# One scores episode per block, two-block first chunks and early weight quarters in a planned attention + MLP kernel

## The chip, the cores and the metric

The kernel runs on one core of one Trainium2 chip. The metric is the device time of one execution in microseconds (us), as the median of several executions, compared with the kernel before on the same chip. A profile's span is about 2 us shorter than the time of the execution. Engines are called as in the profile: PE (TensorE), PEld (its weight loads), DVE (VectorE), ACT (ScalarE), POOL (GpSimd), SP (SyncE, which issues most DMA).

## The reference, cut to what matters

```
B, H, S, D = 8, 8, 576, 64                     # d_model = H*D = 512
scores = q @ k^T / sqrt(D) + alibi;  window of 128 keys, causal
attn   = softmax(scores);  x = attn @ v        # [8, 576, 512]
xn     = (x - mean) / sqrt(var + 1e-6) * g_ln
out    = x + relu(xn @ w_ch1) @ w_ch2          # 512 -> 2048 -> 512
```

There are 4608 tokens, so 36 blocks of 128 tokens. The MLP needs 1152 matmuls with 512 moving columns; all that PE does besides is attention and transposes.

## The kernel before

Per block of 128 tokens: q, k and v are loaded as float32, cast to fp16 on POOL, transposed on PE (8 transposes, "T"), evicted (copied from PSUM to SBUF); scores are computed ("S"; an *episode* is a run of score matmuls with no other work of PE in it), ACT takes the exp, DVE multiplies with a decay mask, PE multiplies with v ("V"), DVE normalises and takes the layer-norm statistics and writes `xs`, PE transposes `xs` ("X") into the chunk's `xt`. Per chunk of four blocks: first layer ("A", 16 tiles of four matmuls), relu on ACT or DVE, second layer ("B", 4 tiles of 16 matmuls), residual, store.

The order of instructions on each engine is fixed when the kernel is built, by a list scheduler in the kernel itself (`Plan`). Every task has assumed costs and a priority; PSUM banks are acquired and released in the plan: four hold the scores (tile `sc`), four (`fb`) serve everything else. At run time each engine works its list in that order. The part that makes the scores:

```python
sc = psum.tile([P, 4, 512], FP32, tag="sc", name="sc")     # four banks, one tile
...
def e_s(half):                                             # 8 matmuls
    def emit(e, b):
        for slot in range(2):
            for side in (() if r == 0 else (0,)) + (1,):
                for g in range(2):
                    nc.tensor.matmul(sc[:, 2 * half + g, c0 : c0 + P], kt[rows, 1, hp, :],
                                     qkt[i][rows, 0, hp, :], start=True, stop=True)   # 64 rows
    return emit
sa  = add(f"Sa{i}", ("PE", 0.38), e_s(0), [ev] + prev, av(i, 2.0), acq=("sa", f"Sa{i}"))
sb_ = add(f"Sb{i}", ("PE", 0.38), e_s(1), [sa] + prev, av(i, 2.0), acq=("sb", f"Sb{i}"))
for half, s_ in ((0, sa), (1, sb_)):
    ...   # exp of that half on ACT: reads sc[:, 2*half : 2*half+2, :]
```

And the part that loads the weights, in four quarters each (float32 to fp16 in the DMA, issued by POOL):

```python
W_AFTER = {0: 4, 1: 8}       # w1 behind the loads of block 3, w2 behind those of block 7
```

The softmax here doesn't subtract the row's maximum and nothing guards it: scores larger than these inputs give would overflow.

## Time and profile before

| | before |
|---|---|
| time | 363.4 us (362.27 to 363.58, 3 runs) |
| span of the profile | 361.1 us |
| PE busy | 332.4 us, 92% |
| first MLP matmul | 34.15 us |
| PE waits for exp in its scores | 6.6 us, 22 times |
| four blocks in steady state | 37.18 us (X of blocks 20 and 24, at 181.88 and 219.06 us); 36.8 us as the mean of six chunks (first-layer starts at 75.15 and 295.70 us) |

The head of the profile page: busy time of each engine, then 40 equal slices of the span, each digit the busy share in tenths.

```profile
PE 332.4 (92%) x2672; PEld 173.4 (48%) x2672; DVE 216.7 (60%) x444; ACT 157.5 (44%) x237; POOL 78.8 (22%) x127
PE   1586999999999999999999999999999999999995
DVE  0578497667658666666657666765676667641011
DMA  9999999999996444564454346441000010002002
```

PE is full from the fifth slice on; what it is not doing lies in the first four slices (36 us), where the DMA engines are full. But a busy PE is not a PE at its peak: the Trainium skill, "Perfetto Trace Analysis", section "Identifying the Most-Contended Engine", calls matmul busy time no good measure of the distance to the roof, because matmuls are pipelined. So the spacing of starts has to be read. The waits of PE, longest in total first (line, waiting for what: us in total, times, longest):

```profile
PE fb L354 <- DMA iden<-iden: 7.3, 1, 7.3
PE sc L380 <- ACT probs L403: 6.6, 22, 0.6
PE fb L423 <- POOL vx L346: 3.1, 1, 3.1
```

The second line is the one that recurs. It is seen in the timeline of PE around one block's scores (start, length, engine, line, what; in brackets the idle time before and who ended it):

```profile
200.46 0.38 PE L519 MATMUL fb<-xt,w1sb 128*128 128x512 f16 x1
200.78 0.23 PE L380 MATMUL sc<-qkt,qkt 64*128 64x128 f16 x2
200.95 0.22 PE L380 MATMUL sc<-qkt 64*128 64x128 f16 x2
201.10 1.04 PE L519 MATMUL fb<-xt,w1sb 128*128 128x512 f16 x4
202.44 0.23 PE L380 MATMUL sc<-qkt,qkt 64*128 64x128 f16 x2 [0.30 <-ACT probs L403]
...
202.78 0.82 PE L519 MATMUL fb<-xt,w1sb 128*128 128x512 f16 x3
```

and of ACT in the same time:

```profile
201.38 1.02 ACT L403 ACTIVATE probs<-sc 128x1024 f16<-128x1024 f32 x1
202.94 1.02 ACT L403 ACTIVATE probs<-sc 128x1024 f16<-128x1024 f32 x1 [0.55 <-PE sc L380]
```

The planner put one first-layer tile (0.86 us of matmuls at 0.216 us each) between the two halves of the scores. PE is through with it at about 201.96 and stands until 202.44, because the exp of the first half, which reads banks 0 and 1 of the tile, ends at 202.40. (The 0.30 us in brackets is shorter because the profile models the ends of matmuls.) The second half writes only banks 2 and 3. The wait is made by the tile, not by the data (e3 below tests that).

### The profile page before, as it was taken

The page shows a single profiled execution, that of the slowest core. Times are in us where ns is not written, and L with a number is a line of the kernel's source. Part 1 is how long each engine was busy: PE and PEld are TensorE (multiplying, and loading weights), DVE is VectorE, ACT ScalarE, POOL GpSimd, SP SyncE. Part 2 cuts the span into 40 slices and gives each one's busy share as a digit, 9 for nine tenths or more (in the row PEclk, how much of TensorE's full clock was granted, in tenths as well). Part 3 has the DMA queues.
Part 4 walks back from the last instruction along what each step waited for, and adds up shares of the span by engine and source line. Part 5 has one row for each costly group of instructions (what it writes and reads, how often), then busy time and mean ns, then how long its engine had stood idle before and what let it go on. Part 6 is the DMA issues. An engine that isn't in the chain of part 4 may idle for free.

```text
span 361.1 us, 6732 instructions
## 1 busy us (share of the span) xinstructions
PE 332.4 (92%) x2672; PEld 173.4 (48%) x2672; DVE 216.7 (60%) x444; ACT 157.5 (44%) x237; POOL 78.8 (22%) x127
## 2 busy tenths in 40 slices
PE   1586999999999999999999999999999999999995
PEld 0364455545545545544554554555455555444442
DVE  0578497667658666666657666765676667641011
ACT  4253576245334542464245433653365335612700
POOL 4851541632112121112101211230111100000000
PEclk9999999999999999999999999999999999999999
DMA  9999999999996444564454346441000010002002
GB/s 169 226 194 212 218 196 208 201 230 224 234 186 196 93 88 124 142 115 93 122 134 93 89 118 145 119 89 56 33 29 2 29 61 31 0 31 87 0 33 86
DMA packets 122384, 42.75 MB, mean 118 GB/s; under 512 B 113392, under 2 KB 117616, under 8 KB 122352
## 3 DMA queue, kind: packets, MB, share of 16 engines
q1 hardware_dynamic: 118128, 38.12, 47.0%
q0 software_dynamic: 4224, 4.19, 7.0%
q8 instruction: 21, 0.34, 0.4%
q14 instruction: 11, 0.09, 0.1%
HBM read 37.06 MB, written 9.44 MB: 129 GB/s over the span
## 4 chain that ended last, share of the span: by engine, by line
PE 80%; ACT 12%; DVE 3%; POOL 2%; DMA 1%; issue 1%; SPq 0%; ACTq 0%; DVEq 0%
PE fb L519 32%; PE fb L545 32%; ACT probs L403 8%; PE sc L380 5%; PE fb L423 5%; PE fb L354 4%; PE fb L480 2%; ACT xt L490 2%; ACT ht L531 1%; DMA k<-in_k_dram 1%; DVE probs L409 1%; DVE xb L443 1%; POOL mmix L290 1%; POOL mnew L290 1%; DVE st L459 1%
## 5 line engine op out<-in xcount | busy, mean ns | idle before, releaser
L519 PE MATMUL fb<-xt,w1sb 128*128 128x512 f16 x576 | 140.7, 383 | 0.0
L545 PE MATMUL fb<-w2sb,ht 128*128 128x512 f16 x576 | 137.7, 379 | 0.0
L531 ACT ACTIVATE ht<-fb 128x512 f16<-128x512 f32 x118 | 70.4, 598 | 75.3 <-PE fb L519 75.1
L403 ACT ACTIVATE probs<-sc 128x1024 f16<-128x1024 f32 (+1 forms) x72 | 69.8, 974 | 37.2 <-PE sc L380 36.9
L519 PEld LDWEIGHTS <-w1sb 128*128 128x128 f16 x576 | 51.3, 98 | 52.9 <-issue 1.4
L545 PEld LDWEIGHTS <-ht 128*128 128x128 f16 x576 | 51.0, 98 | 52.3
L553 DVE SCALAR_TENSOR_TENSOR ot<-fb,rstd,xb 128x512 f32<-128x512 f32 x36 | 26.8, 748 | 46.4 <-PE fb L545 45.3
L346 POOL CAST vx<-v 128x512 f16<-128x512 f32 x36 | 22.6, 631 | 137.7 <-PE fb L423 128.9
L409 DVE TENSOR_TENSOR probs<-probs,mreg 128x1024 f16<-128x1024 f16 (+1 forms) x56 | 37.2, 666 | 24.8 <-ACT probs L403 24.4
L423 PEld LDWEIGHTS <-probs 128*128 128x128 f16 x544 | 26.9, 102 | 20.4 <-DVE probs L409 3.5
L490 ACT ACTIVATE xt<-fb 128x512 f16<-128x512 f16 x20 | 11.9, 597 | 55.1 <-PE fb L480 52.2
L337 POOL CAST q<-q 128x512 f16<-128x512 f32 x36 | 23.5, 653 | 57.1 <-issue 25.1
L380 PEld LDWEIGHTS <-qkt 64*128 64x128 f16 x544 | 19.4, 98 | 31.8 <-issue 24.7
L423 PE MATMUL fb<-vx,probs 128*128 128x65 f16 x544 | 29.9, 200 | 4.4 <-POOL vx L346 3.1
L529 DVE TENSOR_SCALAR ht<-fb 128x512 f16<-128x512 f32 x26 | 18.0, 692 | 24.1 <-PE fb L519 24.1
L380 PE MATMUL sc<-qkt,qkt 64*128 64x128 f16 x256 | 23.0, 229 | 9.4 <-ACT probs L403 6.6
L443 DVE TENSOR_TENSOR xb<-fb,rec 128x256 f16<-128x256 f32 x72 | 30.3, 423 | 2.1
L362 DVE COPY qkt<-fb 128x1024 f16<-128x1024 f16 x36 | 24.7, 686 | 10.4 <-PE fb L354 10.3
L470 DVE SCALAR_TENSOR_TENSOR xs<-xb,mv,g_t 128x512 f16<-128x512 f16 x36 | 28.3, 787 | 1.0
L380 PE MATMUL sc<-qkt 64*128 64x128 f16 x288 | 25.3, 229 | 0.8 <-DVE qkt L362 0.8
L459 DVE BATCH_NORM_STATS2 st<-xb 128x6 f32<-128x512 f16 x36 | 25.0, 694 | 1.1
L337 POOL CAST k<-k 128x512 f16<-128x512 f32 x36 | 23.0, 640 | 8.1 <-DMA k<-in_k_dram 8.0
(28 smaller groups left out, 135.8 us busy)
## 6 DMA issues: line engine op xcount, KB each, us to landing
out_dram<-ot SPq DMA_DIRECT2D x36, 256.0 KB, 2.1
q<-in_q_dram SPq DMA_DIRECT2D x32, 256.0 KB, 4.3
k<-in_k_dram SPq DMA_DIRECT2D x32, 256.0 KB, 4.6
v<-in_v_dram SPq DMA_DIRECT2D x32, 256.0 KB, 4.4
w1sb<-in_moe_w_ch_dram POOLq DMA_DIRECT2D x4, 512.0 KB, 10.9
w2sb<-in_moe_w_ch_dram POOLq DMA_DIRECT2D x4, 512.0 KB, 11.0
q<-in_q_dram SPq DMA_DIRECT2D x8, 128.0 KB, 3.7
k<-in_k_dram SPq DMA_DIRECT2D x8, 128.0 KB, 3.6
```

The costliest lines, as they stand in the source:

```text
L337: en.tensor_copy(out=dst[i][:, :], in_=s)
L380: nc.tensor.matmul(sc[:, 2 * half + g, c0 : c0 + P], kt[rows, 1, hp, :], qkt[i][rows, 0, hp, :], start=True, stop=True,)
L403: nc.scalar.activation(out=o, in_=n_, func=AF.Exp, scale=inv_sqrt_d)
L409: nc.vector.tensor_tensor(out=pv, in0=pv, in1=mask[:, 2 * half : 2 * half + 2, :, lo:], op=ALU.mult)
L423: nc.tensor.matmul(pp[:, hh * (D + 1) : hh * (D + 1) + D + 1], probs[i][:, bank, slot, side * P : side * P + P], vx[i - 1 + side][:, h, 0 ...
L443: nc.vector.tensor_tensor(out=xb[i][:, 256 * half : 256 * half + 256].rearrange("p (h d) -> p h d", d=D), in0=pp[:, :, 0:D], in1=rec[2 * i ...
L459: nc.vector.bn_stats(out=st[i][:, :], in_=xb[i][:, :])
L470: nc.vector.scalar_tensor_tensor(out=xs[i][:, :], in0=xb[i][:, :], scalar=mv[c][:, j, 0:1], in1=g_t[:, :], op0=ALU.subtract, op1=ALU.mult,)
L519: nc.tensor.matmul(fb[b][:, :], w1sb[:, kb, f * P : f * P + P], xt[c][:, kb, :], start=(kb == 0), stop=(kb == NKB - 1),)
L531: nc.scalar.activation(out=ht[c][:, f, :], in_=src, func=AF.Relu)
L545: nc.tensor.matmul(pm[:, :], ht[c][:, f, j * P : j * P + P], w2sb[:, f, :], start=(f == 0), stop=(f == NFB - 1),)
L553: nc.vector.scalar_tensor_tensor(out=ot[i][:, :], in0=fb[plan.held[key][1]][:, :], scalar=rstd[c][:, j : j + 1], in1=xb[i][:, :], op0=ALU. ...
```

## The change

Its intent: compute a block's scores in one episode of 16 matmuls into two PSUM tiles; start the MLP earlier with two chunks of two blocks; issue the weight quarters between the first blocks' loads; allow early casts to be shared among engines. Cut to its core:

```diff
-    NCHUNK = NBLK // CB
+    CHUNKS = [2, 2] + [4] * 8
-    sc = psum.tile([P, 4, 512], FP32, tag="sc", name="sc")
+    scs = [psum.tile([P, 2, 512], FP32, tag=f"sc{n}", name=f"sc{n}") for n in range(2)]
+    PICK = {}
-    W_AFTER = {0: 4, 1: 8}
+    W_AFTER = [2, 2, 3, 3, 4, 5, 6, 7]        # w1 quarters, then w2 quarters
+        (t_w1 if n < 4 else t_w2).append(dma(f"w{n}", "POOL", 0.8, 3.25, emit, loads[i][1], av(i, -60.0))[1])
-        c_eng = {"POOL": 0.62}
+        def pick(name, default, **cost):
+            return {e: cost[e] for e in PICK.get((name, i), default).split()}
-        sa = add(f"Sa{i}", ("PE", 0.38), e_s(0), ..., acq=("sa", f"Sa{i}"))
-        sb_ = add(f"Sb{i}", ("PE", 0.38), e_s(1), ..., acq=("sb", f"Sb{i}"))
+        s_ = add(f"S{i}", ("PE", 0.64 if r else 0.42), e_s, [ev] + prev, av(i, 2.0), acq=("sc", f"S{i}"))
```

Cut away: the mask copies on POOL get a later priority (they end up spread between the first casts), the planner prefers weight DMAs over loads and skips an engine where another would finish earlier, and the costs of small chunks are scaled; a few other assumed costs move by up to 0.1 us. `PICK` is empty, so no cast moves: all 108 of them are on POOL in both kernels.

More of the change, by code (lines that the diff above doesn't have):

```diff
@@ L101, in run @@
                     r, b = at(t)
-                    if r is not None:
-                        cand.append((max(r, f), t.v, t, b))
+                    if r is None:
+                        continue
+                    s = max(r, f)
+                    if any(max(r, free[o]) + c < s + t.eng[e] - 1e-9 for o, c in t.eng.items() if o != e):
+                        continue
+                    cand.append((s, t.v, t, b))
                 if not cand:
@@ L106, in run @@
                 s = min(c[0] for c in cand)
-                c = min((c for c in cand if c[0] <= s + 1e-9), key=lambda c: c[1])
+                c = min((c for c in cand if c[0] <= s + 1e-9), key=lambda c: (c[2].v > -9e3, c[2].ready) if e == "DMA" else c[1])
                 if best is None or (s, c[1]) < (best[0], best[1]):
@@ L163 @@
     CH = CB * P
-    NCHUNK = NBLK // CB
+    CHUNKS = [2, 2] + [4] * 8
+    FIRST = [sum(CHUNKS[:c]) for c in range(len(CHUNKS))]
+    CHUNK_OF = [c for c, n in enumerate(CHUNKS) for _ in range(n)]
     VD = D + 2
@@ L219 @@
     rec = ring("rec", 4, [P, 4], FP32)
-    sc = psum.tile([P, 4, 512], FP32, tag="sc", name="sc")
+    scs = [psum.tile([P, 2, 512], FP32, tag=f"sc{n}", name=f"sc{n}") for n in range(2)]
     fb = {n: psum.tile([P, 512], FP32, tag=f"fb{n}", name=f"fb{n}") for n in range(4)}
-    plan.banks["sa"] = [0]
-    plan.banks["sb"] = [1]
+    plan.banks["sc"] = [0]
     plan.banks["fb"] = list(fb)
@@ L247, in dma @@
         t = add(name + ".i", (eng, issue), emit, deps, v, lat=0.0)
-        return t, add(name, ("DMA", secs), None, [t], v, lat=2.0)
+        return t, add(name, ("DMA", secs), None, [t], -1e4 if eng == "POOL" else v, lat=2.0)
     def load(name, src, r, i, v):
@@ L286 @@
     for dst, lst, name in ((mmix, tmix, "mmix"), (mnew, tnew, "mnew")):
-        vv = av(3, 0.0) - 200
+        vv = av(2, 3.0)
         for hb in range(2):
@@ L297, in z3 @@
         nc.gpsimd.memset(mnew[0:HALF, :, :, 0:P], 0.0)
-    tmix += [add("z1", ("POOL", 0.6), z1, list(tmix), av(3, 0.1) - 200)]
-    tmix += [add("z2", ("POOL", 0.6), z2, tmix[:2], av(3, 0.1) - 200)]
-    tnew += [add("z3", ("POOL", 1.2), z3, list(tnew), av(3, 0.1) - 200)]
+    tmix += [add("z1", ("POOL", 0.6), z1, list(tmix), av(2, 3.1))]
+    tmix += [add("z2", ("POOL", 0.6), z2, tmix[:2], av(2, 3.1))]
+    tnew += [add("z3", ("POOL", 1.2), z3, list(tnew), av(2, 3.1))]
     loads, kept = {}, {}
@@ L309 @@
         )
-    W_AFTER = {0: 4, 1: 8}
+    W_AFTER = [2, 2, 3, 3, 4, 5, 6, 7]
     t_w1, t_w2 = [], []
-    for n in range(4):
+    for n, i in enumerate(W_AFTER):
         def emit(e, b, n=n):
-            nc.gpsimd.dma_start(out=w1sb[:, :, 512 * n : 512 * n + 512], in_=w1r[:, :, 512 * n : 512 * n + 512])
-        t_w1.append(dma(f"w1_{n}", "POOL", 0.9, 3.25, emit, loads[W_AFTER[0] - 1][2], av(W_AFTER[0], 0.5) - 300)[1])
-    for n in range(4):
-        def emit(e, b, n=n):
-            nc.gpsimd.dma_start(out=w2sb[:, 4 * n : 4 * n + 4, :], in_=w2r[:, 4 * n : 4 * n + 4, :])
-        t_w2.append(dma(f"w2_{n}", "POOL", 0.9, 3.25, emit, loads[W_AFTER[1] - 1][2], av(W_AFTER[1], 0.5) - 300)[1])
-    qkt_done, vx_done, aggr_done, xt_done = {}, {}, {}, {}
+            m = n % 4
+            if n < 4:
+                nc.gpsimd.dma_start(out=w1sb[:, :, 512 * m : 512 * m + 512], in_=w1r[:, :, 512 * m : 512 * m + 512])
+            else:
+                nc.gpsimd.dma_start(out=w2sb[:, 4 * m : 4 * m + 4, :], in_=w2r[:, 4 * m : 4 * m + 4, :])
+        (t_w1 if n < 4 else t_w2).append(dma(f"w{n}", "POOL", 0.8, 3.25, emit, loads[i][1], av(i, -60.0))[1])
+    qkt_done, vx_done, aggr_done, xs_done, xt_done = {}, {}, {}, {}, {}
     def attention(i):
@@ L338, in e_cast @@
             return emit
-        c_eng = {"POOL": 0.62}
-        cq = add(f"cq{i}", c_eng, e_cast(q16, q32), lq, av(i, 0.0))
-        ck = add(f"ck{i}", c_eng, e_cast(k16, k32), lk, av(i, 0.1))
+        def pick(name, default, **cost):
+            return {e: cost[e] for e in PICK.get((name, i), default).split()}
+        cq = add(f"cq{i}", pick("cq", "POOL", POOL=0.62, ACT=0.6, DVE=0.35), e_cast(q16, q32), lq, av(i, 0.0))
+        ck = add(f"ck{i}", pick("ck", "POOL", POOL=0.62, ACT=0.6, DVE=0.35), e_cast(k16, k32), lk, av(i, 0.1))
         q32.reads(i, cq); k32.reads(i, ck); q16.writes(i, cq); k16.writes(i, ck)
         def e_cv(e, b):
-            nc.gpsimd.tensor_copy(out=vx[i][:, :, 0:D], in_=v32[i][:, :, :])
-        cv = add(f"cv{i}", ("POOL", 0.66), e_cv, lv_, av(i, 0.2))
+            if e == "ACT":
+                nc.scalar.activation(out=vx[i][:, :, 0:D], in_=v32[i][:, :, :], func=AF.Copy)
+            else:
+                nc.gpsimd.tensor_copy(out=vx[i][:, :, 0:D], in_=v32[i][:, :, :])
+        cv = add(f"cv{i}", pick("cv", "POOL", POOL=0.64, ACT=0.62), e_cv, lv_, av(i, 0.2))
         v32.reads(i, cv); vx.writes(i, cv)
@@ L364, in e_ev @@
                 nc.scalar.activation(out=dst, in_=src, func=AF.Copy)
-        ev = add(f"ev{i}", {"DVE": 0.7}, e_ev, [tt], av(i, 1.2), rel=f"T{i}")
+        ev = add(f"ev{i}", pick("ev", "DVE", DVE=0.7, ACT=1.02), e_ev, [tt], av(i, 1.2), rel=f"T{i}")
         qkt.writes(i, ev)
@@ L369, in attention, with e_s @@
         prev = [] if r == 0 else [qkt_done[i - 1]]
-        def e_s(half):
-            def emit(e, b):
+        def e_s(e, b):
+            for half in range(2):
                 for slot in range(2):
@@ L380, in emit @@
                             nc.tensor.matmul(
-                                sc[:, 2 * half + g, c0 : c0 + P],
+                                scs[half][:, g, c0 : c0 + P],
                                 kt[rows, 1, hp, :],
@@ L386, in emit @@
                             )
-            return emit
         pr = []
-        sa = add(f"Sa{i}", ("PE", 0.38), e_s(0), [ev] + prev, av(i, 2.0), acq=("sa", f"Sa{i}"))
-        sb_ = add(f"Sb{i}", ("PE", 0.38), e_s(1), [sa] + prev, av(i, 2.0), acq=("sb", f"Sb{i}"))
-        for half, s_ in ((0, sa), (1, sb_)):
-            qkt.reads(i, s_)
-            if r:
-                qkt.reads(i - 1, s_)
+        s_ = add(f"S{i}", ("PE", 0.64 if r else 0.42), e_s, [ev] + prev, av(i, 2.0), acq=("sc", f"S{i}"))
+        qkt.reads(i, s_)
+        if r:
+            qkt.reads(i - 1, s_)
+        for half in range(2):
             def e_x(e, b, half=half):
                 o = probs[i][:, 2 * half : 2 * half + 2, :, lo:]
-                n_ = sc[:, 2 * half : 2 * half + 2, :].rearrange("p b (s c) -> p b s c", s=2)[:, :, :, lo:]
+                n_ = scs[half][:, :, :].rearrange("p b (s c) -> p b s c", s=2)[:, :, :, lo:]
                 if r:
                     o = o.rearrange("p b s c -> p b (s c)")
-                    n_ = sc[:, 2 * half : 2 * half + 2, :]
+                    n_ = scs[half][:, :, :]
                 nc.scalar.activation(out=o, in_=n_, func=AF.Exp, scale=inv_sqrt_d)
-            ex = add(f"ex{'ab'[half]}{i}", ("ACT", 1.03 if r else 0.62), e_x, [s_], av(i, 2.4 + half), rel=f"S{'ab'[half]}{i}")
+            ex = add(f"ex{'ab'[half]}{i}", ("ACT", 1.02 if r else 0.62), e_x, [s_], av(i, 2.4 + half), rel=f"S{i}")
             probs.writes(i, ex)
@@ L408, in e_m @@
                 pv = probs[i][:, 2 * half : 2 * half + 2, :, lo:]
-                nc.vector.tensor_tensor(out=pv, in0=pv, in1=mask[:, 2 * half : 2 * half + 2, :, lo:], op=ALU.mult)
-            pr.append(add(f"mk{'ab'[half]}{i}", ("DVE", 0.69 if r else 0.42), e_m, [ex] + t_mask, av(i, 3.0 + half)))
+                en = nc.vector if e == "DVE" else nc.gpsimd
+                en.tensor_tensor(out=pv, in0=pv, in1=mask[:, 2 * half : 2 * half + 2, :, lo:], op=ALU.mult)
+            pr.append(add(f"mk{'ab'[half]}{i}", pick("mk" + "ab"[half], "DVE", DVE=0.69 if r else 0.42, POOL=1.4 if r else 0.8), e_m, [ex] + t_mask, av(i, 3.0 + half)))
         vx_done[i] = cv
@@ L454, in attention @@
             nm.append(n_)
-        c, j = i // CB, i % CB
+        c = CHUNK_OF[i]
+        j = i - FIRST[c]
         def e_bn(e, b):
@@ L473, in e_xs @@
             )
-        xs_ = add(f"xs{i}", ("DVE", 0.69), e_xs, [ag, d_g], av(i, 6.6))
+        xs_ = add(f"xs{i}", ("DVE", 0.75), e_xs, [ag, d_g], av(i, 6.6))
         xs.writes(i, xs_)
+        xs_done[i] = xs_
         def e_tx(e, b):
@@ L490, in e_xt @@
                 nc.scalar.activation(out=dst, in_=src, func=AF.Copy)
-        xt_ = add(f"xt{i}", {"ACT": 0.6, "DVE": 0.45}, e_xt, [tx], av(i, 7.6), rel=f"TX{i}")
+        xt_ = add(f"xt{i}", pick("xt", "ACT DVE", ACT=0.6, DVE=0.45), e_xt, [tx], av(i, 7.6), rel=f"TX{i}")
         xt.writes(c, xt_)
         xt_done[i] = xt_
-        if j == CB - 1:
-            ag4 = [aggr_done[c * CB + n] for n in range(CB)]
+        if j == CHUNKS[c] - 1:
+            ag4 = [aggr_done[FIRST[c] + n] for n in range(CHUNKS[c])]
+            nb = CHUNKS[c]
             def e_ln(e, b):
-                nc.scalar.activation(out=lv[c][:, :], in_=mv[c][:, :, 1], func=AF.Ln, bias=eps_t[:, :])
+                nc.scalar.activation(out=lv[c][:, 0:nb], in_=mv[c][:, 0:nb, 1], func=AF.Ln, bias=eps_t[:, :])
             def e_rs(e, b):
-                nc.scalar.activation(out=rstd[c][:, :], in_=lv[c][:, :], func=AF.Exp, scale=-0.5)
+                nc.scalar.activation(out=rstd[c][:, 0:nb], in_=lv[c][:, 0:nb], func=AF.Exp, scale=-0.5)
             ln = add(f"ln{c}", ("ACT", 0.3), e_ln, ag4, av(i, 9.0))
@@ L505, in attention @@
             lv.writes(c, ln); lv.reads(c, rs); mv.reads(c, ln); rstd.writes(c, rs)
-            for n in range(CB):
-                mv.reads(c, xs_)
+            for n in range(nb):
+                mv.reads(c, xs_done[FIRST[c] + n])
             kept[c] = rs
     def mlp(c):
-        done = [xt_done[c * CB + n] for n in range(CB)]
+        nb = CHUNKS[c]
+        n_ = nb * P
+        done = [xt_done[FIRST[c] + n] for n in range(nb)]
+        v0, per = FIRST[c] / CB * SPAN, nb / CB * SPAN / 32
         relu = []
@@ L514, in mlp @@
             key = f"A{c}.{f}"
-            vm = c * SPAN + f * SPAN / 32
+            vm = v0 + f * per
             def e_a(e, b, f=f):
@@ L519, in e_a @@
                     nc.tensor.matmul(
-                        fb[b][:, :], w1sb[:, kb, f * P : f * P + P], xt[c][:, kb, :],
+                        fb[b][:, 0:n_], w1sb[:, kb, f * P : f * P + P], xt[c][:, kb, 0:n_],
                         start=(kb == 0), stop=(kb == NKB - 1),
                     )
-            a = add(key, ("PE", 0.864), e_a, done + [t_w1[f // 4]], vm, acq=("fb", key))
+            a = add(key, ("PE", 0.216 * nb), e_a, done + [t_w1[f // 4]], vm, acq=("fb", key))
             xt.reads(c, a)
             def e_r(e, b, f=f, key=key):
-                src = fb[plan.held[key][1]][:, :]
+                src = fb[plan.held[key][1]][:, 0:n_]
                 if e == "DVE":
-                    nc.vector.tensor_scalar(out=ht[c][:, f, :], in0=src, scalar1=0.0, scalar2=None, op0=ALU.max)
+                    nc.vector.tensor_scalar(out=ht[c][:, f, 0:n_], in0=src, scalar1=0.0, scalar2=None, op0=ALU.max)
                 else:
-                    nc.scalar.activation(out=ht[c][:, f, :], in_=src, func=AF.Relu)
-            r_ = add(f"r{c}.{f}", {"ACT": 0.6, "DVE": 0.69}, e_r, [a], vm - 4.0, rel=key)
+                    nc.scalar.activation(out=ht[c][:, f, 0:n_], in_=src, func=AF.Relu)
+            r_ = add(f"r{c}.{f}", {"ACT": 0.17 + 0.107 * nb, "DVE": 0.16 + 0.133 * nb}, e_r, [a], vm - 4.0, rel=key)
             ht.writes(c, r_)
             relu.append(r_)
-        for j in range(CB):
-            i = c * CB + j
+        for j in range(nb):
+            i = FIRST[c] + j
             key = f"B{i}"
@@ L539, in mlp @@
             for f0 in range(0, NFB, 4):
-                vm = c * SPAN + (16 + 4 * j + f0 / 4) * SPAN / 32
+                vm = v0 + 16 * per + (4 * j + f0 / 4) * SPAN / 32
                 def e_b(e, b, j=j, f0=f0, key=key):
@@ L556, in e_o @@
                 )
-            o = add(f"o{i}", ("DVE", 0.69), e_o, [last, kept[c]], vm - 4.0, rel=key)
+            o = add(f"o{i}", ("DVE", 0.75), e_o, [last, kept[c]], vm - 4.0, rel=key)
             ot.writes(i, o); rstd.reads(c, o); xb.reads(i, o)
@@ L566 @@
         attention(i)
-    for c in range(NCHUNK):
+    for c in range(len(CHUNKS)):
         mlp(c)
```

## The prediction

> **What bounds it now.** TensorE. The busy table gives PE 332.4 of 361.1 us (92%), DVE 60%, ACT 44%. The timeline shows two regimes. Until 34.15 us no MLP matmul runs: PE waits (waits of PE: 7.3 us for the identity, 3.1 for a POOL cast of v, 4.8 for DVE), while the stretches table shows the DMA engines full to 80 us. From then PE streams to 357.4; the tail after it is 3.7 us.
>
> In steady state four blocks cost 36.8 us (first-layer matmuls at 75.3 and 295.9 us, six chunks). 128x512 matmuls start 0.216 us apart, so 128 of them are 27.6. Per block the timeline shows transposes 0.45, probabilities times v 0.48, transposes of xs 0.23, and scores in two episodes of eight: each costs 0.34 plus a 0.1 gap on entry, and the second starts 1.2 to 1.34 us after a 0.86 us filler, because it waits for the first half's exp (22 waits of PE scores on ACT, 6.6 us). Both halves are in one PSUM tile, so the second write waits for a read of other banks.
>
> **What changes.** (1) Two tiles, 16 score matmuls in a row: estimated from these gaps 0.65 us instead of 1.10 to 1.26, so 0.5 us per block, all on the critical path. Some 27 blocks lie behind 75 us: 13 to 14 us. ACT then does two exps of 1.02 us back to back; DVE and four banks should carry the relus.
> (2) First chunks of two blocks: the first layer can start at about 21 us instead of 34.
> (3) Weight quarters come earlier, behind query casts. DMA is the limit here. Before, four quarters issued at 18.4 to 20.8 us landed 6.7 to 14.9 us later, about 3.6 us each, and a q load issued meanwhile took 15.0 instead of 4.5 us. The Trainium skill, "DMA: Bandwidth & Descriptors", section "Issuing engines are not separate DMA queues", says that such DMAs share 16 engines; this trace agrees. All weights (29 us) and eight blocks (3.55 us each) need until about 58 us. The instruction order has w2's last quarter issued only behind block 7's query cast, and the first two output tiles' last accumulation before the first four-block chunk. I expect that quarter near 57 us and that chunk's first matmul near 70 us, against 75.3 before, with 1.3 us less attention done: 3 to 4 us gained of the 13 us earlier start.
> (4) The shared casts do nothing: the table of picks is empty, all 108 casts stay on POOL. Its mask copies are spread, which brings block 1 forward 3 us.
>
> PE may run cold between waits: the Trainium skill, "TensorE: Matmul & The Clock Gate", "What's actually happening", says that the array runs at half clock after about 3.4 us idle. The trace agrees: first-layer matmuls at 34.3 us started 0.43 us apart. I allow 1 to 2 us.
>
> **Predicted: 345 us** (343 span + 2), range 336 to 353; faster by over 2%: 0.92, within 2%: 0.07, slower: 0.01.
>
> **Right if** waits of PE scores on ACT fall from 6.6 to under 1 us; a steady four-block period is 34.8 to 35.3 us; the first layer starts at 20 to 25 us; new PE waits of 8 us or more for w1, w2 or late loads appear before 60 us; 128x512 first-layer matmuls start at 67 to 73 us.
>
> **Wrong if** DMA shares loads and weights better (that chunk at 62 us: about 337); if doubled exps starve the bank evictions (period above 36: 352); or if entering and leaving score episodes costs less than I read.

## The result, and the profile after

The change took 346.7 us (345.6 to 347.81, 4 runs) against 362.95 us before in the same rounds. Ratios here are the mean time of one kernel's fast runs over that of the other's of the same rounds, so not quite the ratio of the medians: 0.9553, with a 95% interval of 0.9515 to 0.959. Timed again later in five rounds (e12 below) it took 347.97 us, ratio 0.9577 (0.9557 to 0.9597).

The head of the page after:

```profile
PE 321.2 (93%) x2736; PEld 177.8 (52%) x2736; DVE 217.1 (63%) x454; ACT 153.1 (44%) x245; POOL 80.7 (23%) x127
PE   1488788999999999999999999999999999999995
DVE  0885686897867666766676667666766676631011
DMA  9999999999999535644473456431100110011011
```

PE has 64 more matmuls (the small chunks) and 11 us less busy time, for the same work. Slices 5 to 7 (34 to 60 us) are less full than before. The waits of PE, all but four short ones:

```profile
PE fb L364 <- DMA iden<-iden: 7.1, 1, 7.1
PE fb L491 <- DVE xs L480: 4.5, 3, 2.3
PE sc L390 <- DVE qkt L372: 2.8, 5, 0.9
PE fb L432 <- DVE probs L418: 2.4, 2, 1.4
PE fb L534 <- DMA w1sb<-in_moe_w_ch_dram: 0.8, 1, 0.8
```

No line says that scores wait for ACT any more, and one wait of 0.8 us is all that PE is shown to spend on weights directly. One block's scores in the steady state, PE and then ACT:

```profile
199.56 0.39 PE L491 MATMUL fb<-iden,xs 128*128 128x128 f16 x4
199.88 0.23 PE L390 MATMUL sc<-qkt,qkt 64*128 64x128 f16 x2
...
200.28 0.22 PE L390 MATMUL sc<-qkt 64*128 64x128 f16 x2
200.43 2.76 PE L560 MATMUL fb<-w2sb,ht 128*128 128x512 f16 x12
```

```profile
200.48 1.93 ACT L411 ACTIVATE probs<-sc 128x1024 f16<-128x1024 f32 x2
```

The episode takes 0.65 us of PE (199.78, where the transposes end at 0.0556 us each, to 200.43), of which 0.10 is a gap on entry and 0.09 one on exit. Before, the two episodes and their gap took 1.24 us of it (2.00 us from 200.78 to 202.78, less the tile of 0.86, plus the first entry gap of 0.1). Both exps follow each other. Four blocks now take 34.89 us (X of blocks 18 and 22, at 155.09 and 189.98 us). Periods differ from block to block; over six chunks (first-layer starts at 71.05 and 279.34 us) the mean is 34.7 us against 36.8 before, which is 0.5 us per block.

**A ledger.** To see where time goes across kernels I use one derived number. Let work be the number of PE instructions started, each times its warm spacing read from the timeline: 0.2157 us for 512 columns, 0.108 for 256, 0.0556 for a transpose, 0.0344 for a score matmul, 0.0302 for one with v. It sums to 307.6 us in every correct kernel here. Lost time is elapsed time minus that work. The last column is part of the lost time and an estimate: the work that was started while TensorE ran at half clock, and so took about twice as long. It is taken from the clock records of each trace. Before a trace's first record there is none, and there transposes start 0.107 us apart in every run, so that time is counted as half clock too. It is an upper bound of what the half clock cost, because PE may have had to wait anyway. By stretch, in us:

| run | time, us | ratio to before (95%) | lost 0-20 | 20-40 | 40-80 | 80-300 | of it half clock |
|---|---|---|---|---|---|---|---|
| before | 363.4 | 1 | 16.9 | 11.2 | 3.6 | 16.5 | 9.5 |
| the change | 346.7 | 0.9553 (0.9515-0.959) | 16.3 | 8.2 | 5.3 | 3.1 | 6.7 |
| e12 the change again | 347.97 | 0.9577 (0.9557-0.9597) | 16.3 | 9.0 | 6.1 | 3.3 | 9.1 |
| e1 scores alone | 347.6 | 0.9577 (0.9559-0.9594) | 16.5 | 11.7 | 2.0 | 3.8 | 8.5 |
| e2 scores alone, one tile | 348.14 | 0.9582 (0.9567-0.9597) | 16.2 | 12.6 | 2.1 | 3.6 | 8.2 |
| e3 two tiles, two episodes | 353.54 | 0.9735 (0.972-0.9749) | 16.4 | 10.6 | 3.2 | 9.1 | 6.9 |
| e4 the start alone | 367.62 | 1.0117 (1.0094-1.014) | 17.2 | 9.3 | 9.1 | 17.6 | 7.8 |
| e5 change, chunks of four | 349.07 | 0.9607 (0.958-0.9633) | 16.3 | 14.7 | 1.1 | 3.2 | 8.5 |
| e6 change, late weights | 345.32 | 0.9503 (0.9479-0.9527) | 16.3 | 7.9 | 4.7 | 3.1 | 7.5 |
| e7 half weights (wrong result) | 346.1 | 0.9524 (0.9476-0.9573) | 16.3 | 9.0 | 5.3 | 3.2 | 8.5 |
| e8 weights first, four small chunks | 353.82 | 0.9731 (0.968-0.9781) | 16.9 | 7.2 | 11.9 | 4.4 | 9.0 |
| e9 half weights, planned (wrong result) | 342.73 | 0.9438 (0.9421-0.9455) | 16.3 | 4.8 | 4.5 | 3.6 | 3.7 |
| e10 change, ACT evictions | 347.88 | 0.9569 (0.9535-0.9602) | 16.9 | 8.8 | 4.4 | 3.2 | 6.3 |
| e11 late weights, ACT evictions | 345.27 | 0.9511 (0.9488-0.9533) | 16.3 | 6.9 | 6.4 | 2.9 | 6.4 |

The ledger of the change against before: of 16.6 us, 13.4 come from the steady stretch, 1.3 from what lies after 300 us (with the last blocks' scores), and 1.9 from all of the first 80 us, although the first layer begins at 22.62 us instead of 34.15. In e12, the same kernel timed again, it is 0.3 us, and its half-clock estimate is 2.4 us above that of the first profile: executions of one kernel differ by that much at the start.

### The profile page after: what moved, and what is told of

It is laid out like the page before. It is cut to its first block, busy times and chain, and to the rows that moved or that the text cites. A ratio compares the mean times of both kernels' runs of the same rounds, so it can differ in the third digit from the quotient of the medians.

```text
span 344.6 us, 6879 instructions
## 1 busy us (share of the span) xinstructions
PE 321.2 (93%) x2736; PEld 177.8 (52%) x2736; DVE 217.1 (63%) x454; ACT 153.1 (44%) x245; POOL 80.7 (23%) x127
## 4 chain that ended last, share of the span: by engine, by line
PE 87%; DMA 5%; POOL 2%; DVE 2%; SPq 1%; issue 1%; ACT 0%; DVEq 0%
PE fb L560 36%; PE fb L534 35%; PE sc L390 5%; PE fb L432 4%; DMA w1sb<-in_moe_w_ch_dram 4%; PE fb L364 4%; PE fb L491 2%; DMA k<-in_k_dram 1%; POOL w1sb L323 1%; SPq L260 1%; POOL mnew L296 1%; DVE qkt L372 0%; POOL vx L356 0%; POOL k L343 0%; DVE ht L544 0%
## 5 line engine op out<-in xcount | busy, mean ns | idle before, releaser
L534 PE MATMUL fb<-xt,w1sb 128*128 128x512 f16 (+1 forms) x640 | 140.8, 363 | 1.7 <-DMA w1sb<-in_moe_w_ch_dram 0.8
L546 ACT ACTIVATE ht<-fb 128x512 f16<-128x512 f32 (+1 forms) x136 | 76.1, 562 | 77.2 <-PE fb L534 75.7
L411 ACT ACTIVATE probs<-sc 128x1024 f16<-128x1024 f32 (+1 forms) x72 | 66.4, 975 | 68.3 <-PE sc L390 68.3
L534 PEld LDWEIGHTS <-w1sb 128*128 128x128 f16 x640 | 59.8, 99 | 54.2 <-issue 1.5
L432 PEld LDWEIGHTS <-probs 128*128 128x128 f16 x544 | 25.0, 99 | 15.6 <-DVE probs L418 3.5
L544 DVE TENSOR_SCALAR ht<-fb 128x512 f16<-128x512 f32 (+1 forms) x24 | 14.1, 589 | 26.4 <-PE fb L534 26.3
L432 PE MATMUL fb<-vx,probs 128*128 128x65 f16 x544 | 27.4, 196 | 2.7 <-DVE probs L418 2.4
L448 DVE RECIPROCAL rec<-fb 128x4 f32<-128x4 f32 x72 | 12.7, 180 | 23.3 <-PE fb L432 21.9
L390 PEld LDWEIGHTS <-qkt 64*128 64x128 f16 x544 | 16.3, 97 | 14.1 <-issue 10.2
L364 PE MATMUL fb<-iden,q 128*128 128x128 f16 x144 | 14.8, 229 | 7.1 <-DMA iden<-iden 7.1
L390 PE MATMUL sc<-qkt 64*128 64x128 f16 x288 | 20.4, 224 | 0.8 <-DVE qkt L372 0.8
```

What stands on the lines that cost most here:

```text
L364: nc.tensor.transpose(pt[:, a, hp, :], s[i][:, hp * P : hp * P + P], iden[:, :])
L390: nc.tensor.matmul(scs[half][:, g, c0 : c0 + P], kt[rows, 1, hp, :], qkt[i][rows, 0, hp, :], start=True, stop=True,)
L411: nc.scalar.activation(out=o, in_=n_, func=AF.Exp, scale=inv_sqrt_d)
L432: nc.tensor.matmul(pp[:, hh * (D + 1) : hh * (D + 1) + D + 1], probs[i][:, bank, slot, side * P : side * P + P], vx[i - 1 + side][:, h, 0 ...
L534: nc.tensor.matmul(fb[b][:, 0:n_], w1sb[:, kb, f * P : f * P + P], xt[c][:, kb, 0:n_], start=(kb == 0), stop=(kb == NKB - 1),)
L546: nc.scalar.activation(out=ht[c][:, f, 0:n_], in_=src, func=AF.Relu)
```

## The experiments

My theory was that one scores episode brings 13 to 14 us, and the start 3 to 4 us, with DMA as the limit of the start. Rivals: that the earlier first layer is the main gain; and, within the scores, that either the split of the tile or the number of episodes is what counts.

### e1_scores: the scores part alone

```diff
 # the kernel before
-    sc = psum.tile([P, 4, 512], ...)          # one tile
-    Sa (8 matmuls) ... Sb (8 matmuls)
+    scs = [psum.tile([P, 2, 512], ...) ...]   # two tiles
+    S (16 matmuls)
```

> The kernel before with the scores part of the change alone: two PSUM tiles and one episode of 16 score matmuls per block; chunks, weights and mask copies as before. My theory (score episodes are worth about 0.5 us for each of the blocks behind the start-up, on TensorE's own chain) expects 348 to 351 us, 12 to 15 us less than before, no waits of PE scores on ACT, and a four-block period near 35.0 us. The rival, that the earlier start of the first layer brings most of the gain, expects 357 us or more here.

Measured: 347.6 us, ratio 0.9577, 15.6 us less than the 363.19 of its rounds, and no wait of scores on ACT. That is all of the change's gain within the noise: e12, the change itself in five rounds, has the same ratio. The gain is a little over the upper end of what I expected for it. In the ledger 12.7 us of it lie between 80 and 300 us, as costed; 1.5 us lie before 80 us, where I had counted nothing.

### e2_one_tile: one episode, tile not split

```diff
 # e1_scores
-    scs[half][:, g, c0 : c0 + P]
+    sc[:, 2 * half + g, c0 : c0 + P]          # one tile of four banks, as before
```

> As e1_scores, with the same order of instructions on TensorE, but the 16 score matmuls go into the one PSUM tile of four banks as before. Inside an episode nothing reads the tile, so if the gain comes from having one episode (my theory: no wait for the first half's exp in the middle, and one entry and exit instead of two), this is 348 to 352 us, within 1 us of e1_scores. The rival, that the tile must be split to lose the false dependence, expects waits of PE scores on ACT to remain near 6 us and 357 us or more.

Measured: 348.14 us, ratio 0.9582. The order of PE's instructions is that of e1, and the times are the same within the noise. Splitting the tile is not needed once there is a single episode: then nothing reads the tile while it is written.

### e3_two_tiles: the split alone

```diff
 # the kernel before, order of instructions on PE unchanged
-    sc[:, 2 * half + g, c0 : c0 + P]
+    scs[half][:, g, c0 : c0 + P]              # Sa and Sb stay two episodes
```

> The kernel before with its order of instructions on TensorE unchanged (two episodes of eight), but the two halves in two PSUM tiles. The false wait goes, the second entry and exit stay. If both cost something, this lies between: 354 to 358 us, waits of PE scores on ACT near 0, period near 36. If the wait is all, 349 us as e1_scores; if only the number of episodes counts, 362 us or more.

Measured: 353.54 us, no wait of scores on ACT. One block's scores on PE:

```profile
186.34 1.04 PE L519 MATMUL fb<-xt,w1sb 128*128 128x512 f16 x4
187.31 0.23 PE L380 MATMUL sc<-qkt,qkt 64*128 64x128 f16 x2
187.38 0.22 PE L380 MATMUL sc<-qkt 64*128 64x128 f16 x2
187.44 0.22 PE L380 MATMUL sc<-qkt,qkt 64*128 64x128 f16 x2
187.49 0.22 PE L380 MATMUL sc<-qkt 64*128 64x128 f16 x2
187.64 1.69 PE L519 MATMUL fb<-xt,w1sb 128*128 128x512 f16 x7
```

The second half now starts 0.97 us after the tile before it, 0.10 more than that tile's work, where it started 1.34 us after it before; and the next tile starts about 0.09 after the scores' last pair. In time, the 15.6 us part into 9.65 us for the false wait (363.19 to 353.54) and 5.9 us for the second entry and exit (353.54 to 347.6), which is 0.165 us for each of 36 blocks, next to the two gaps of 0.10 and 0.09. The split is not exact: the plan orders other work differently in e1, and in the stretch from 80 to 300 us alone the two parts are 7.4 and 5.3 us. The Trainium skill, "TensorEngine Tiling (Array Packing)", section "Key Properties", says that changing the tiling mode drains TensorE; the scores use 64 rows of the array and all else uses 128. The gaps agree with it. No run here separates the drain from other costs of the switch.

### e4_start: the start-up part alone

```diff
 # the changed kernel
-    two tiles, S (16 matmuls)
+    one tile, Sa (8 matmuls), Sb (8 matmuls)
```

> The changed kernel with the scores put back (one tile, two episodes): the start-up part alone, two chunks of two blocks, early weight quarters, spread mask copies. My theory (DMA bounds the start, so only 3 to 4 us remain of a first layer that starts 11.5 us earlier) expects 357 to 361 us. The rival, that the earlier first layer pays in full, expects 349 to 353 us.

Measured: 367.62 us, 4.4 us slower than before. Both theories missed. Most of that is lost before 80 us: 35.6 against 31.7 us in the ledger. Two of its three longest waits (the third is the one for the identity, as in every run):

```profile
PE sc L391 <- ACT probs L414: 10.3, 25, 0.8
PE fb L435 <- DVE probs L421: 5.6, 4, 2.6
```

The start-up part alone is a loss with the old scores and nothing that these runs can show with the new ones. The rest of the experiments ask why.

### e5_chunks4 and e6_late_weights: the two halves of the start

```diff
 # the changed kernel, e5
-    CHUNKS = [2, 2] + [4] * 8
+    CHUNKS = [4] * 9
 # the changed kernel, e6
-    W_AFTER = [2, 2, 3, 3, 4, 5, 6, 7]
+    W_AFTER = [3, 3, 3, 3, 7, 7, 7, 7]
```

> The changed kernel with nine chunks of four blocks as before, but early weights, spread mask copies and new scores kept. The scores-only kernel took 347.6 us and the whole change 346.7, so the start-up part is worth about 1 us in all. If the small first chunks are what fills TensorE while weights and loads compete, early weights alone delay blocks 3 to 7 and this is slower than scores alone: 349 to 352 us. The rival, that early weights carry the small gain and the chunks nothing, expects 346 to 347.

> The changed kernel with the weights issued where they were (w1 behind block 3, w2 behind block 7), small first chunks and new scores kept. The first layer can then not start before about 25 to 30 us, and TensorE runs out of first-layer work before w2 lands at 50 to 60 us. If start-up is bound by the sum of DMA and its order matters little, 346 to 349 us. If early weights are needed for small chunks, 350 us or more.

Measured: e5 349.07 us, e6 345.32 us. With e1 and the change this is nearly a two by two table (e1 has the old places of the mask copies, the old planner rule and the old assumed costs besides; e6 issues its weights behind the k loads of blocks 3 and 7, the kernel before behind their v loads): late weights and chunks of four 347.6, early and four 349.1, late and two 345.3, early and two 346.7 and 348.0. The small first chunks gain 1 to 2.4 us, the early weight quarters cost 1.4 to 2.7 us, whichever way the other is set. The interval of e6 and that of e12 do not touch, and neither do those of e11 (late weights, below) and e12. The pair e5 against e1 alone would not settle it, because their intervals overlap. For the small chunks the only pair without overlap is e6 against e1, which differ in the other things too; e5 against e12, the clean pair, overlaps by a little. Early weights delay the loads they were put between: in the change the two q loads of block 4 land at 30.2 and 31.7 us, in e6 at 20.0 and 20.6. The q load of block 5 lands at 35.2 us in the one and 35.1 in the other. e6 and e11 (345.27 us) are also the fastest correct kernels here, ahead of both kernels: e6 is ahead of the change by 0.4 to 0.8%, with an interval that just overlaps the first measurement of the change and is clear of the second.

### e7_half_weights: take away half of the weight DMA

```diff
 # the changed kernel; the result is wrong on purpose
-    dma_start(out=w1sb[:, :, 512*m : 512*m + 512], ...)
+    dma_start(out=w1sb[:, :, 512*m : 512*m + 256], ...)      # w2: 2 of 4 row blocks
+    nc.vector.memset(the other halves, 0.0)                  # at the start, on DVE
```

> The changed kernel with the same order of instructions on TensorE, but every weight DMA moves half its columns; the other half is set to zero at the start (the result is wrong on purpose). That takes about 14 us of the DMA's 57 us away and nothing from TensorE. If DMA bounds the start-up (my theory), TensorE's lost time falls by 5 to 8 us: 338 to 342 us, with w2 landing before 50 us. If the fixed order of instructions or DVE and ACT latency bound it (the rival), 345 us or more.

Measured: 346.1 us, no gain that the intervals show. But its four executions spread from 343.73 to 347.56 us: two (343.73 and 344.91) lie below all nine of the change, whose fastest took 345.6, and the profiled one (347.29) is not among them. A gain of 1 or 2 us is not excluded. The weights did come earlier: the last quarter of w2 landed at 45.2 us instead of 57.6. PE's timeline did not follow. The change, then e7, from 48 us on:

```profile
48.17 0.65 PE L432 MATMUL fb<-vx,probs 128*128 128x65 f16 x16
49.47 2.10 PE L534 MATMUL fb<-xt,w1sb 128*128 128x256 f16 x16 [0.65 <-DVE xb L452]
53.07 0.23 PE L390 MATMUL sc<-qkt,qkt 64*128 64x128 f16 x2 [0.63 <-DVE qkt L372]
...
71.05 1.03 PE L534 MATMUL fb<-xt,w1sb 128*128 128x512 f16 x4
```

```profile
49.04 0.65 PE L435 MATMUL fb<-vx,probs 128*128 128x65 f16 x16
50.34 2.10 PE L537 MATMUL fb<-xt,w1sb 128*128 128x256 f16 x16 [0.65 <-DVE xb L455]
53.94 0.23 PE L393 MATMUL sc<-qkt,qkt 64*128 64x128 f16 x2 [0.63 <-DVE qkt L375]
...
71.91 1.03 PE L537 MATMUL fb<-xt,w1sb 128*128 128x512 f16 x4
```

The same instructions with the same waits, 0.86 to 0.87 us apart throughout. (The start of e7 has eight memsets on DVE more, and its TensorE reached full clock at 27.90 us instead of 24.37.) So from 48 us on it was not the arrival of w2 that set the pace of the changed kernel; what stayed the same is the order of instructions with the chains between engines in it. This contradicts the step of my prediction that had the last quarter of w2 as the gate of the first four-block chunk.

### e8_weights_first: an attempt to beat both

```diff
 # the changed kernel
+    W_AFTER = [2, 2, 2, 2, 3, 3, 3, 3]
+    CHUNKS = [2, 2, 2, 2] + [4] * 7
```

> An attempt to beat both: all weight quarters in a row behind blocks 2 and 3, and four chunks of two blocks, so that TensorE can work through four blocks of MLP while the loads of blocks 4 to 7 follow. If the order of DMA decides what TensorE has to do before 60 us, 337 to 343 us. If the order matters little, 345 to 348; the risk is that second-layer matmuls that wait for w2 stand ahead of the attention of block 3 in the fixed order, 350 or more.

Measured: 353.82 us, slower than the change. The risk named came true. The planner, which lets weights go ahead of all loads, put the whole second layer of the first chunk ahead of block 3's product with v, and PE stood for w2 where it had attention to do:

```profile
PE fb L560 <- DMA w2sb<-in_moe_w_ch_dram: 6.2, 4, 2.4
```

Lost time from 40 to 80 us is 11.9 us here, against 5.3.

### e9_half_planned: tell the planner

```diff
 # e7_half_weights
-    dma(f"w{n}", "POOL", 0.8, 3.25, ...)
+    dma(f"w{n}", "POOL", 0.8, 1.7, ...)
```

> e7 (half of every weight DMA, wrong result on purpose) gained nothing and its TensorE timeline from 40 to 72 us was that of the changed kernel, 0.9 us late. Here the planner is told that a weight quarter takes 1.7 us of DMA instead of 3.25, so the fixed order of instructions changes too. If the order made for slow weights was what held e7 back, while DMA is the limit behind it, TensorE's lost time up to 80 us falls by 4 us or more: 337 to 342 us. If DVE and latency bound the first blocks whatever the order (DVE is busy 9.7 of the 10 us from 10 to 20 us), 343 us or more.

Measured: 342.73 us, ratio 0.9438, just outside the range for "order, with DMA behind it" and inside its other criterion: lost time up to 80 us is 25.6 us, 4.2 less than in the change. The bytes alone gave nothing that the intervals show, bytes and the order planned for them together gave 4 us. That DMA limits the start through the plan that was made for it would fit, but it is not shown, for two reasons. No run has e9's order with all of the bytes, so the order alone may be what gains; e6, another order with all bytes, already gains 1.4 us or more. And the clock differs: in e9 TensorE reaches full clock at 19.68 us and keeps it to the end of its work, in the change it reaches it at 24.37 us and loses it again from 38.02 to 41.44. The half-clock estimate is 3.7 us against 6.7, so up to 3 of the 4.2 us can be clock. All four executions of e9 lie within 0.7 us and show a mean clock of 0.999 or more, so its clock is hardly luck; a PE that waits less may be what keeps it.

### e10_act_evictions and e11_late_act: relieve DVE in the first blocks

DVE is busy 9.70 of the 10 us from 10 to 20 us in the change, and the waits of PE in that time name DVE. So the table of picks was filled, in the change (e10) and in e6 (e11):

```diff
-    PICK = {}
+    PICK = {(n, i): "ACT" for n, blocks in (("ev", (1, 2, 3)), ("xt", (0, 1, 2))) for i in blocks}
```

> The changed kernel with its table of picks filled: the PSUM evictions of the transposes of blocks 1 to 3 and of xs of blocks 0 to 2 go to ACT (busy 2.5 of 10 us there) instead of DVE, about 3.3 us of DVE work. If DVE's serial work per block bounds the first 25 us, X of block 1 comes 1 us or more earlier and the time falls by 1 to 2 us: 344 to 346 us. If DMA or the order of later instructions bounds the start, no change: 346 to 348 us.

> e6 (weights where they were) took 345.3 us. With the same ACT evictions as e10: 343.5 to 345 us if DVE bounds the first blocks, 345 to 346.5 us if not. Beside it the question whether late weights are at least as good as the early quarters of the change: then this is again below 346.7 us.

Measured: 347.88 and 345.27 us, no gain in either. Lost time up to 20 us is 16.9 us in e10 against 16.3 in the change, with DVE still busy 9.02 of 10 us from 10 to 20. X of block 1, which was to come 1 us earlier, starts at 21.63 us against 21.50; in e11 it does come earlier (20.53 against 22.17 in e6), and the time is the same. Moving six evictions of DVE's work is not enough, or not the right part. Whether DVE bounds the first blocks is left open.

### e12_change_again

> The changed kernel itself, unchanged, timed again in five rounds, to place it against the same change with the weights issued late (ratios to the kernel before 0.9503 and, with ACT evictions, 0.9511). If the early weight quarters cost something, as the pair e5 against e1 says too (349.1 against 347.6 us), the ratio is 0.954 to 0.957 with an interval that does not reach 0.951. If the two are the same, it falls to 0.951 to 0.953.

Measured: 347.97 us, ratio 0.9577 with an interval from 0.9557. That is just above the range expected if early weights cost something, and away from 0.951. Over scores alone (e1) the start-up part is worth nothing that these runs can show.

## Why the prediction was right or wrong

- **Time: right.** 345 us predicted, 346.7 measured, 348.0 the second time; the range was 336 to 353. Part of that is luck: the scores gave about 2 us more than predicted and the start-up part about 3 us less, and the two nearly cancel.
- **Scores: right in mechanism and size.** Predicted 13 to 14 us behind 75 us; the ledger has 14.7 us behind 80 us for the whole change and 13.8 for the scores alone. Waits on ACT went from 6.6 us to none, the episode costs the 0.65 us estimated, and the four-block period is 34.89 us in the window shown (34.8 to 35.3 predicted); measured as the prediction measured it before, over six chunks, it is 34.7 us, just below that range. What I left out is 1.5 us from the blocks before 80 us, so that the scores part alone gives 15.6 us. "Two tiles" was named beside the 16 matmuls in a row; e2 shows that the single episode alone does it, while e3 shows what the tile split does without it.
- **First layer earlier: right, and worth less than said.** It starts at 22.62 us (20 to 25 predicted). With the mask copies spread block 1 comes forward: its scores start at 12.86 instead of 15.71 us (13.86 in e12).
- **"3 to 4 us gained of the 13 us earlier start": wrong.** Measured: nothing within the noise over scores alone, and 4.4 us lost with the old scores. The term is made of 1 to 2.4 us gained by the small chunks and 1.4 to 2.7 us lost by the early weight quarters.
- **"I expect that quarter near 57 us and that chunk's first matmul near 70 us": right numbers, wrong reason.** The quarter landed at 57.6 us and the matmul started at 71.05 us. But e7 lands it at 45.2 us and starts the matmul at 71.91. The two times were near each other without one making the other.
- **"New PE waits of 8 us or more for w1, w2 or late loads": wrong.** 0.8 us waited directly on w1. From 20 to 60 us PE waits mostly on DVE (2.3 us in one wait for `xs` of block 3, whose product with v stood behind first-layer matmuls in PE's order), and its lost time of 12.3 us holds much that no wait shows: an estimated 3.1 us of it is half clock.
- **Clock: seen, and larger than allowed.** Two stretches of the change, from 25 us and behind that wait of 2.3 us:

```profile
25.02 1.47 PE L534 MATMUL fb<-xt,w1sb 128*128 128x256 f16 x12
37.78 3.40 PE L534 MATMUL fb<-xt,w1sb 128*128 128x256 f16 x16
```

  The 16 first-layer matmuls of the second line took 3.20 us (37.78 to 40.98) instead of 1.73. The Trainium skill, "TensorE: Matmul & The Clock Gate", section "What's actually happening", has a cold array at half clock; 0.20 us each against 0.108 agrees. That is 1.5 us, within the 1 to 2 allowed, but it is not all: TensorE is at half clock before 24.37 us too, and the whole comes to an estimated 6.7 us (9.1 in e12), against 9.5 before. The trace bears out the half rate, not the 3.4 us idle that the prediction names with it: these 14 traces hold 12 falls to half clock before 330 us, and in the 6 us before each no idle time of PE had lasted longer than 2.4 us.
- **Shared casts do nothing: right** for an empty table; and the filled one of e10 does nothing either.

Open: what bounds the first 40 us. Less weight traffic with another order gains 4 us, other orders lose up to 6, a lighter DVE gains nothing. The half clock, which the experiments did not control, is an estimated 3.7 to 9.5 us of the lost time, and e9 and e12, 5.2 us apart in time, are 5.4 us apart in that estimate. No one of DMA, DVE, order and clock has been shown to be the bound alone.

## What to carry to other kernels

On an engine that works its list in order, a short episode that is split in two pays twice: once for the gap at each change of array mode, and once for whatever waits get between the halves; look for the wait that data does not need before costing anything else. When an order is fixed at build time for assumed arrivals, earlier arrivals may gain nothing until the order is planned again, so test a suspected limit both with the old order and with a new one. Where TensorE stands often, read its clock records beside the waits before a loss is put down to DMA or order. An earlier first start is not a gain by itself: count the work done by the time the bottleneck is full, in both kernels.

## What the Trainium skill lacked or had wrong

- "TensorEngine Tiling (Array Packing)", "Key Properties", gives no figure for the drain at a change of mode. Here a change from 128-row matmuls to 64-row ones left a gap of about 0.10 us, back again about 0.09 us, and a second episode per block cost 5.9 us over 36 blocks (e3 against e1, whose plans differ in the order of other work too).
- "DMA: Bandwidth & Descriptors", "Queues, rings and completion order", says that engines go round between queues by packets, and gives no share for a large casting DMA of GpSimd beside small loads. Here, while four weight quarters landed 3.5 us apart before the change, a q load took 15.0 us instead of 4.5.
- "TensorE: Matmul & The Clock Gate", "Seeing it yourself", warns that the clock gate's events in a trace can be unreliable. Here they were not: between the change's records of 38.02 us (half) and 41.44 us (full) matmuls of 256 columns start 0.213 us apart, in full clock 0.109. What misleads is their absence: the granted clock of the stretches reads 1.00 from 0 to 20 us, where transposes start about 0.107 us apart instead of 0.056, because the change's first record is at 24.37 us. No page says that a trace holds no record before the first change.
